# From the tenth pair on, a pair's value products and lane sums issued as one run on TensorE, under a new table of ranks

## The chip, the cores and the metric

One core of one Trainium2 chip runs the whole program. The metric is the device time of one execution in microseconds (us). TensorE (PE) does the matrix products, with a separate weight load (PEld) that overlaps them; VectorE (DVE), ScalarE (ACT) and GpSimd (POOL) do the elementwise work, SyncE (SP) issues every transfer.

## The reference

Four batches of twelve attention heads (448 tokens, 64 columns each) with a soft cap on the scores, then two dense layers with a squared ReLU between them on all 1792 tokens:

```
scores = cap * tanh(scale * q @ k.T / cap)
attn   = exp(scores) / (sum(exp(scores)) + 1e-9)
x      = (attn @ v), heads side by side            # 1792 x 768
h      = x @ w_in                                   # 768 -> 2048
g      = s * relu(h)**2 + b
out    = g @ w_out                                  # 2048 -> 768
```

The weights arrive as float64 and are brought to float32 in the kernel (L655 to L659).

## The kernel before

Heads go in pairs: 4 batches x 6 pairs, 24 in all. A key axis of 448 is cut into three chunks of 128 and a rest of 64; the rests of two neighbouring pairs share a fourth chunk. `scores` (L505) multiplies the keys of one chunk with all queries of both heads of a pair, two matmuls of 64 rows (four for the shared chunk), in f32; ACT takes the tanh out of PSUM (L509) and the exponential in place (L513). Two PSUM buffers (`ps_s`) hold such chunks. `pv` then multiplies the exponentials with the values: for each key chunk four matmuls of 32 columns (L563), and two groups of four that sum the exponentials over the keys with a matrix of ones (L571). One PSUM buffer (`ps_v`) takes these; ACT empties it (L591). Five small transfers, POOL and DVE then turn the sums into a normalised and scaled x, whose largest value is summed over lanes by a small product on PE (L470, once a batch). In the code names below, pair (b, c) is pair c of batch b.

The first dense layer (`m1`, L835 to L837, three f16 products for each f32 one) needs all six pairs of its batch; the second (`m2`, L1086 to L1088) follows. For the last two batches both go by a scheme with fewer products (`m1pair`, `m2pair`, L995). Weight tiles are prepared on the way: `win` does a w_in tile (column sums on PE at L705, a maximum on DVE at L713 to L715, a lane sum at L470, scales at L721 to L726, conversions at L426 to L429, remainders at L446). `wout` does a w_out column tile (maximum at L451, sums on POOL and DVE at L436 and L437, the bias product L778 on PE, a lane sum at L470, scales, a split at L429 and L446 and a transfer away, L819).

The order on every engine is made when the program is built. Each piece of work is entered as an operation with an engine (or several to choose from), a length, a rank, what it reads and what it writes; an entry `at` in the table `CHOICE` gives each unit (a double pair, a weight tile, a column tile of a layer) its rank and step. `emit` then plays the operations through, engine by engine: among the ones at the head of a queue it takes the one that could start first, prefers on PE the kind of the last one (`kind`: 1 and 3 scores, 2 values), and is bounded by `cling`; `bias`, `late` and `lag` are further numbers of that choice. The order that comes out is fixed; at run time each engine works in its own order and waits on semaphores.

An operation of `pv` is one such piece. `parts` says which key chunks go into one: chunks 0 and 1 with the first sums are the first, chunks 2 and 3 with the last sums the second.

## Time and profile before

| | |
|---|---|
| median of 3 runs | 646.98 us (643.51 to 649.58) |
| profiled execution | 644.03 us, span 642.2 us |
| PE busy | 627.1 us, 98% of the span |
| DVE, ACT, POOL busy | 397.6, 326.6, 273.8 us |
| mean granted clock of TensorE | 0.997 |
| moved by DMA | 101.67 MB |

A busy PE in this profile is not PE at its peak: a matmul's record runs on while the next has begun. How fast PE goes is therefore read from starts to starts, as the chain of waits gives them.

### The profile page before, as it was taken

What the parts mean: (1) busy time and instruction counts of PE and PEld (TensorE: products, weight loads), DVE (VectorE), ACT (ScalarE), POOL (GpSimd) and SP (SyncE); (2) the same over time, 40 slices, a digit from 0 to 9 for tenths busy, and PEclk for the clock granted to TensorE, in tenths of its full rate; (3) what the DMA queues carried; (4) which work ended last, traced back from release to release, by engine and by line L of the source; (5) the groups of instructions that cost most, each with busy time, mean ns of one, the idle gap of its engine ahead of it and who ended that gap; (6) DMA issues with size and microseconds to landing.
All of it is one profiled execution on the core that took longest, in us unless ns stands there. A gap on an engine that the chain in (4) does not pass through costs nothing.

```text
span 642.2 us, 11452 instructions
## 1 busy us (share of the span) xinstructions
PE 627.1 (98%) x4404; PEld 331.4 (52%) x4404; DVE 397.6 (62%) x778; ACT 326.6 (51%) x423; POOL 273.8 (43%) x319
## 2 busy tenths in 40 slices
PE   6999999999999999999999999999999999999997
PEld 2333344443334443333544445555558997556997
DVE  5896789997487787787400584745976222666222
ACT  5999987467866547537353561435544001434100
POOL 4553446885566568566343851112834001221000
PEclk9999999999999999989999999999999999999999
DMA  7767355441465674672800216676502875000672
GB/s 289 282 206 216 104 160 157 131 142 47 133 201 153 219 260 122 226 245 83 288 27 1 93 43 234 242 277 212 210 2 68 256 259 168 25 2 3 217 255 72
DMA packets 54775, 101.67 MB, mean 158 GB/s; under 512 B 16193, under 2 KB 34753, under 8 KB 54721
## 3 DMA queue, kind: packets, MB, share of 16 engines
q1 hardware_dynamic: 54720, 100.95, 47.1%
q8 instruction: 34, 0.56, 0.3%
q14 instruction: 21, 0.16, 0.1%
HBM read 82.58 MB, written 18.17 MB: 157 GB/s over the span
## 4 chain that ended last, share of the span: by engine, by line
PE 77%; DVE 8%; DMA 7%; POOL 3%; issue 2%; SPq 1%; ACT 0%; POOLq 0%; ACTq 0%
PE ps_m L995 9%; PE ps_s L505 7%; PE ps_s L995 6%; PE ps_v L563 6%; PE ps_s L836 6%; PE ps_s L837 6%; PE ps_s L835 6%; PE ps_m L1086 5%; PE ps_m L1088 5%; PE ps_m L1087 5%; PE ps_m L835 4%; PE ps_m L837 4%; PE ps_m L836 4%; PE ps_v L571 3%; DMA w<-in_w_in 2%
## 5 line engine op out<-in xcount | busy, mean ns | idle before, releaser
L995 PEld LDWEIGHTS <-w 128*128 128x128 f16 x1008 | 96.6, 98 | 0.7
L509 ACT ACTIVATE bed<-ps_s,arena 128x896 f32<-128x896 f32 x84 | 81.6, 1007 | 16.0 <-PE ps_s L505 14.8
L505 PE MATMUL ps_s<-bed 64*128 64x448 f32 (+1 forms) x384 | 82.7, 590 | 3.3 <-DMA bed<-in_qT 2.6
L513 ACT ACTIVATE bed<-bed,par 128x896 f32<-128x896 f32 x84 | 84.5, 1041 | 0.4
L563 PE MATMUL ps_v<-bed 128*32 128x448 f32 x768 | 82.2, 545 | 0.2 <-ACT pw L591 0.2
L1086 PE MATMUL ps_m<-gt,w 128*128 128x448 f16 x192 | 67.7, 353 | 0.0
L835 PE MATMUL ps_m<-x,w 128*128 128x448 f16 x192 | 67.7, 353 | 0.0
L836 PE MATMUL ps_s<-x,w 128*128 128x448 f16 x192 | 67.7, 352 | 0.0
L1088 PE MATMUL ps_m<-gt,w 128*128 128x448 f16 x192 | 67.7, 352 | 0.0
L837 PE MATMUL ps_m<-x,w 128*128 128x448 f16 x192 | 67.7, 352 | 0.0
L1087 PE MATMUL ps_m<-gt,w 128*128 128x448 f16 x192 | 67.7, 352 | 0.0
L835 PE MATMUL ps_s<-x,w 128*128 128x448 f16 x192 | 67.7, 352 | 0.0
L837 PE MATMUL ps_s<-x,w 128*128 128x448 f16 x192 | 67.7, 352 | 0.0
L836 PE MATMUL ps_m<-x,w 128*128 128x448 f16 x192 | 67.7, 352 | 0.0
L835 PEld LDWEIGHTS <-w 128*128 128x128 f16 x384 | 37.6, 98 | 38.7 <-issue 4.2
L837 PEld LDWEIGHTS <-w 128*128 128x128 f16 x384 | 37.6, 98 | 35.1
L836 PEld LDWEIGHTS <-w 128*128 128x128 f16 x384 | 37.6, 98 | 33.7
L429 POOL TENSOR_SCALAR w<-w 128x512 f32<-128x512 f32 x42 | 35.0, 833 | 40.0 <-DVE w L656 31.9
L930 ACT ACTIVATE pw<-ps_s,arena 128x448 f32<-128x448 f32 x32 | 20.3, 633 | 60.9 <-PE ps_s L837 57.8
L505 PEld LDWEIGHTS ps_s<-bed 64*128 64x128 f32 (+1 forms) x384 | 27.3, 177 | 45.4 <-issue 15.8
L437 POOL TENSOR_TENSOR pw<-pw 128x224 f32<-128x224 f32 x16 | 13.7, 860 | 79.5 <-ACT pw L934 63.1
L563 PEld LDWEIGHTS ps_v<-bed 128*32 128x32 f32 x768 | 20.5, 109 | 52.4 <-issue 38.6
(138 smaller groups left out, 1065.3 us busy)
## 6 DMA issues: line engine op xcount, KB each, us to landing
w<-w SPq DMA_DIRECT2D x48, 512.0 KB, 5.5
w<-in_w_out SPq DMA_DIRECT2D x24, 512.0 KB, 5.5
w<-ws SPq DMA_DIRECT2D x24, 512.0 KB, 4.7
w<-in_w_in SPq DMA_DIRECT2D x18, 512.0 KB, 5.4
bed<-in_v SPq DMA_DIRECT2D x24, 256.0 KB, 3.5
ws<-w SPq DMA_DIRECT2D x12, 512.0 KB, 2.9
bed<-in_kT SPq DMA_DIRECT2D x24, 224.0 KB, 3.8
bed<-in_qT SPq DMA_DIRECT2D x24, 224.0 KB, 3.8
```

What stands on the lines that cost most here:

```text
L429: 0.1 + n * 0.00107, lambda: nc.gpsimd.tensor_scalar(dst(), src(), sc, 1.0, ALU.mult, ALU.mult)
L505: nc.tensor.matmul(P[kp][o, h, 0:S], keys, P[q][rows], start=True, stop=True)
L509: 1.01, rank, lambda: nc.scalar.activation(P[kh], P[kp][:, :, 0:S], AF.Tanh, scale=tsc[:, 0:1]),
L513: 1.04, rank, lambda: nc.scalar.activation(P[kh], P[kh], AF.Exp, scale=par[:, 0:1]), r=["par"], w=[kh],
L563: nc.tensor.matmul(P[kp][o, 0, 0:S], P[kv][:, c, o], prob(c, h), start=(c == 0), stop=(c == NC))
L835: nc.tensor.matmul(ps[:, 0:S], wh, x[:, 0], start=(c == 0), stop=False)
L836: nc.tensor.matmul(ps[:, 0:S], wh, x[:, 1], start=False, stop=False)
L837: nc.tensor.matmul(ps[:, 0:S], wl, x[:, 0], start=False, stop=(c == NP - 1))
L995: nc.tensor.matmul(at(), w(g, zw), b(g, zb), start=g == 0 and x == 0, stop=g == n - 1 and x == 2,)
L1086: nc.tensor.matmul(ps[:, 0:S], wh, ghi[:, f], start=(f == 0), stop=False)
L1087: nc.tensor.matmul(ps[:, 0:S], wh, glo[:, f], start=False, stop=False)
L1088: nc.tensor.matmul(ps[:, 0:S], wl, ghi[:, f], start=False, stop=(f == NF - 1))
```

## The change

From the tenth pair on (`early` is 9; pairs are counted batch by batch), `pv` enters one operation with all four key chunks and both groups of sums instead of two operations. It waits in the planner for the pair's last exponential, and nothing can come between its matmuls. For the first nine pairs the two parts stay. The table of ranks and the numbers `bias`, `late`, `lag` and `cling` are new throughout, so that the order on all engines changes:

```diff
 CHOICE = {
-    'bias': 1.798,
+    'bias': 1.543,
...
-        ('a', 0, 0): (-15.1, 72.6), ('a', 0, 2): (69.2, 7.69), ('a', 0, 4): (78.0, 15.05), ('a', 1, 0): (600.1, 1.25),
+        ('a', 0, 0): (-102.1, 106.63), ('a', 0, 2): (99.7, 0.26), ('a', 0, 4): (189.0, 27.49),
...
-    'late': 0.56,
-    'lag': 0.0,
-    'cling': 21.776,
+    'late': 0.358,
+    'lag': 0.047,
+    'cling': 19.384,
     'parts': ((0, 1), (2, 3)),
+    'early': 9,
...
-        for part in CHOICE["parts"]:
+        for part in CHOICE["parts"] if bb * NP + c2 < CHOICE["early"] else (range(NC + 1),):
             both = part[0] == 0
```

Three places in the order show what it moves. In the rows below a line number of the changed kernel is one higher than that of the same line before (L506 for L505, and so on). The first is PE's queue where the first two pairs of the fourth batch (pairs (3, 0) and (3, 1)) get their values, ahead of the second batch's lane sum (the L470 or L471 row). Before:

```order
L505 MATMUL ps_s<-bed 128x448 x4
L563 MATMUL ps_v<-bed 32x448 x8
L571 MATMUL ps_v<-bed,ones 32x448
L571 MATMUL ps_v<-bed,half 32x448
L571 MATMUL ps_v<-bed,ones 32x448
L571 MATMUL ps_v<-bed,half 32x448
L505 MATMUL ps_s<-bed 128x448 x4
L563 MATMUL ps_v<-bed 32x448 x8
L571 MATMUL ps_v<-bed,ones 32x448 x4
L505 MATMUL ps_s<-bed 128x448 x2
L563 MATMUL ps_v<-bed 32x448 x8
L571 MATMUL ps_v<-bed,ones 32x448
```

and now:

```order
L506 MATMUL ps_s<-bed 128x448 x4
L564 MATMUL ps_v<-bed 32x448 x16
L572 MATMUL ps_v<-bed,ones 32x448 x5
L572 MATMUL ps_v<-bed,half 32x448
L572 MATMUL ps_v<-bed,ones 32x448
L572 MATMUL ps_v<-bed,half 32x448
L506 MATMUL ps_s<-bed 128x448 x8
L564 MATMUL ps_v<-bed 32x448 x16
L572 MATMUL ps_v<-bed,ones 32x448 x5
...
L471 LDWEIGHTS ones_132
L471 MATMUL ps_m<-brief,ones_132 128x1
```

The values of a pair stand in one piece of 16 and 8 matmuls, the scores between two pairs in one of 8 matmuls (four chunks), where halves of values and one or two chunks took turns; in the order before, the lane sum stands four rows and one more chunk behind the last row shown.

The second place is ACT's queue at the same point, where pair (3, 0)'s values are taken out of PSUM (L592; L591 before). Before:

```order
L509 ACTIVATE bed<-ps_s,arena 128x896 x2
L513 ACTIVATE bed<-bed,par 128x896 x2
L591 ACTIVATE pw<-ps_v 128x896
L509 ACTIVATE bed<-ps_s,arena 128x896 x2
L513 ACTIVATE bed<-bed,par 128x896 x2
L509 ACTIVATE bed<-ps_s,arena 128x896
L513 ACTIVATE bed<-bed,par 128x896
L591 ACTIVATE pw<-ps_v 128x896
L509 ACTIVATE bed<-ps_s,arena 128x896
L513 ACTIVATE bed<-bed,par 128x896
```

and now:

```order
L510 ACTIVATE bed<-ps_s,arena 128x896 x2
L514 ACTIVATE bed<-bed,par 128x896 x2
L592 ACTIVATE pw<-ps_v 128x896
L510 ACTIVATE bed<-ps_s,arena 128x896 x2
L514 ACTIVATE bed<-bed,par 128x896 x2
L510 ACTIVATE bed<-ps_s,arena 128x896
L514 ACTIVATE bed<-bed,par 128x896
L510 ACTIVATE bed<-ps_s,arena 128x896
L592 ACTIVATE pw<-ps_v 128x896
```

Between the two emptyings (pairs (3, 0) and (3, 1)) stand the tanh of four chunks now, of three before, and in both orders the first emptying comes ahead of them.

The third place is DVE's queue where a w_in tile's maximum follows the tile before it (the lane sum on PE waits for the CAST to `brief`). Before:

```order
L726 TENSOR_SCALAR arena<-arena 128x1
L659 SCALAR_TENSOR_TENSOR w<-w 128x512
L446 SCALAR_TENSOR_TENSOR w_3_124<-w,arena,w_3_124 128x512 x3
L713 TENSOR_REDUCE arena<-ps_m 128x1
L714 TENSOR_SCALAR arena<-arena 128x1
L715 CAST brief<-arena 128x1
```

and now:

```order
L727 TENSOR_SCALAR arena<-arena 128x1
L428 TENSOR_SCALAR w_3_124<-w,arena 128x512 x2
L447 SCALAR_TENSOR_TENSOR w_3_124<-w,arena,w_3_124 128x512 x3
L714 TENSOR_REDUCE arena<-ps_m 128x1
L715 TENSOR_SCALAR arena<-arena 128x1
L716 CAST brief<-arena 128x1
```

The maximum is that of tile 5 before and of tile 2 now; two conversions of tile 3, which ACT did, stand in DVE's queue ahead of it in the place of a step of another tile.

## Rows read from the trace of the kernel before

**Rows 1.** The page, busy time, share of the span and instructions of each engine

```profile
PE 627.1 (98%) x4404; PEld 331.4 (52%) x4404; DVE 397.6 (62%) x778; ACT 326.6 (51%) x423; POOL 273.8 (43%) x319
```

**Rows 2.** Waits of PE: tile and line, whom for: us, times, longest us

```profile
PE ps_s L505 <- DMA bed<-in_qT: 2.6, 2, 1.9
PE ps_m L778 <- POOL bed L437: 2.5, 1, 2.5
...
PE ps_m L470 <- DVE brief L610: 1.6, 2, 1.4
...
PE ps_m L470 <- DVE brief L715: 0.8, 2, 0.5
```

**Rows 3.** Chain of waits, two stretches: start us, us until the next step

```profile
248.13 1.71 PE ps_s L505 x8
249.84 1.64 PE ps_v L563 x16
...
252.23 1.50 PE ps_v L563 x16
...
281.52 0.29 PE ps_m L1086
281.82 0.19 PE ps_m L1087
```

**Rows 4.** Windows: stretch, length, busy us of PE, PEld, DVE, ACT, POOL, PEclk

```profile
0.00:160.00 160.00, 152.18 (x1123) 59.33 (x1127) 130.55 (x264) 123.62 (x154) 90.65 (x109) 1.00 0.53 174
0.00:300.00 300.00, 288.20 (x2070) 113.04 (x2071) 237.42 (x493) 209.02 (x248) 180.05 (x226) 0.99 0.55 180
```

**Rows 5.** Chain of waits behind 274 us, and the window of 276 to 280

```profile
274.72 3.27 PE ps_s L505 x12
277.99 1.82 PE ps_v L563 x16
...
276.00:280.00 4.00, 4.00 (x28) 1.18 (x28) 3.73 (x9) 2.97 (x4) 3.83 (x7) 0.71 0.38 109
```

**Rows 6.** Timeline: start us, us, instruction [idle before, and for whom]

```profile
105.66 1.00 ACT L509 ACTIVATE bed<-ps_s,arena 128x896 f32<-128x896 f32 x1
106.72 1.02 PE L505 MATMUL ps_s<-bed 64*128 64x448 f32 x4 [0.58 <-ACT bed L509]
...
181.48 0.92 ACT L591 ACTIVATE pw<-ps_v 128x896 f32<-128x896 f32 x1 [0.38 <-PE ps_v L571]
```

**Rows 7.** Timeline of DVE at w_in tiles 3 and 5, and a group by line

```profile
99.49 0.14 DVE L721 COPY arena<-ps_m 128x1 f32<-128x1 f32 x1
...
102.64 0.68 DVE L659 SCALAR_TENSOR_TENSOR w<-w 128x512 int32<-128x512 int32 x1
...
106.68 0.16 DVE L715 CAST brief<-arena 128x1 bf16<-128x1 f32 x1
...
L427 DVE TENSOR_SCALAR w<-w,arena 128x512 f16<-128x512 f32 x7 | 3.2, 491 | 0.0
```

**Rows 8.** Chain of waits, the bias products of w_out from the second on

```profile
199.70 0.31 PE ps_m L778 x2
...
224.13 0.31 PE ps_m L778 x2
...
247.72 0.38 PE ps_m L778 x2
...
274.31 0.38 PE ps_m L778 x2
...
300.54 0.31 PE ps_m L778 x2
```

**Rows 9.** Timeline of the start, SP's queue and PE

```profile
3.54 0.44 SPq L1132 DMA_DIRECT2D par<-in_s  x1
...
4.71 0.65 SPq L481 DMA_DIRECT2D bed<-in_kT  x1
...
12.50 0.97 PE L505 MATMUL ps_s<-bed 64*64 64x448 f32 x4 [1.93 <-DMA bed<-in_qT]
```

58 rows, old and new, of the table CHOICE are left out of this document.

## The prediction

> **What bounds the kernel now.** I read four views. The page's table of engines first: TensorE (PE) is busy for 627.1 of 642.2 us [rows 1], the others for at most 62%. So this kernel ends when PE has worked through its queue, and a change of order can only move what PE loses between matmuls. Second, PE's waits [rows 2]: the longest entry is 2.6 us, and that is the start (L505 for q); four entries make 7.6 us. That seems to leave little. Third, the chain of waits, where each step runs to the start of the next [rows 3]: it shows a loss that "busy" hides. Two score chunks take 1.71 us, and the first half of a value run behind them (L563, two key chunks) takes 1.64; the same half straight behind another half takes 1.50 [rows 3]. So each block of values that follows something else pays 0.14. A value step (one key chunk, four column quarters at once) and a score chunk (two row halves at once) stream the same 448 columns in two passes, so I read half of 1.50, 0.75, for either where nothing changes, and each block of scores pays 1.71 - 1.50 = 0.20. Full-width f16 products run at 0.19 apiece, and the first one behind scores shows 0.29: 0.10 [rows 3]. Fourth, the windows: ScalarE (ACT) is busy 123.6 of the first 160 us, VectorE (DVE) 237.4 of the first 300 [rows 4]. These two set when scores and weights are ready.
>
> **The switches.** No matmul is added or removed: 576 of L563/L571, 192 of L505, 1728 f16 of full width and 1008 of half width stand in both orders. What changes is the number of blocks, counted in PE's order: value blocks 44 to 32, score blocks 51 to 41, blocks of f16 products 17 to 18. At the prices above: 12 x 0.14 = 1.7, plus 10 x 0.20 = 2.0, minus 0.1: **-3.6 us**. The bounds are 0, if what I take for a switch is a wait that comes back elsewhere, and these 3.6.
>
> **Waits that lose their place.** The longest one in mid-run is 2.45 us before the bias product L778 at 274.31, for POOL [rows 2, 8]. Behind it the granted clock is 0.71 in 276 to 280 us, a mean of stretches at 2.4 and 1.2 GHz; two score chunks take 3.27 instead of 1.71 and a first half of values 1.82 instead of 1.64 [rows 3, 5]: 2.45 + 1.56 + 0.18 = 4.2. The lane sums of the batches wait 1.6 (L610, 1.4 of it the second batch's), those of the weight tiles 0.8 (L715) [rows 2], a score chunk 0.58 for its buffer [rows 6]. Sum 4.2 + 1.6 + 0.8 + 0.6 = **-7.2** if all of them go. The second batch's lane sum has a better place now: 54 f16 products (10.3 us), two whole value runs (9.3) and seven score chunks lie between its last pair and it, some 26 us by the prices above, where in the order before they come to 20 us. What may come in the place of the other waits is priced in the next parts; none of it at all would be worth 0, and keeping all of them 7.2.
>
> **Score runs of four.** With the values in one run, four score chunks now stand in a row at four places (three times 8 matmuls of L505 between two value runs, once 2 + 4 + 4 with the shared fourth chunk among them, behind a bias product). Score buffers are two. ACT empties a value buffer in 0.92 and does a tanh in 1.00 [rows 6], and at these places its order has the emptying first. What scores do that must wait for a buffer is in the trace once: a tanh ends at 106.66, the scores start at 106.72 after 0.58 of idling [rows 6]. Worked out from the end of a value run, with ACT 0.2 behind it (an estimate from the 0.38 of idling in that row, which counts from its own last instruction): emptying until 1.1, first tanh until 2.05, second until 3.0. The third chunk, due at 1.7, starts at 2.1; the fourth, due then at 2.85, at 3.05. So 0.6 us a run, four runs: **+2.4**. Bounds: 0 if the emptying is done earlier, 1.05 a run (4.2) if ACT comes half a microsecond later. I take 0.6, as the row of the one such wait gives 0.58. The Trainium skill, page "TensorEngine Tiling", section "PSUM Bottleneck", says that tiling quickens TensorE but not the emptying of PSUM, which may then be the limit. Taken at its word (each of the four chunks at ACT's pace, 0.92 + 4 x 1.00 = 4.9 against 3.2) this would be 1.7 a run and 6.8 in all, so a sum 4.4 us higher; the trace speaks for less, since PE waits for ACT's tanh hardly anywhere.
>
> **Lane sums behind less.** The lane sum of weight tile 2 stands now two score chunks behind its column sums, and DVE reaches its maximum only after finishing tile 3: from the first step of a tile's scales to the end of the next tile's maximum DVE took 99.49 to 106.84 in the trace, 7.35 us, with one step of another tile in it (0.68); in the new order two conversions (0.98) stand there in its place [rows 7]: 7.65 us. PE has 18 products (3.4), the column sums (0.4) and two chunks (1.7) to do: 5.5. That is a wait of 2.1 at most, and none if the scales run quicker than there (they took some 3 of the 7.35); **+1.2**, near the middle, as no row is nearer to one end.
>
> **The weights' pitch.** Each column tile of w_out passes load, DVE, POOL, bias product and a DVE/POOL split before the next one gets its buffers. Bias products follow each other in the trace by 24.4, 23.6, 26.6 and 26.2 us [rows 8]; only the 26.6 ended in a long wait. In the new order PE's own work between the last four is summed by the prices above (48 products 9.2, a value run 4.6, a run of four chunks with its wait 3.8, two chunks 1.7, one 0.95, the bias product and its lane sum 0.3): 3.8 + 9.2 + 4.6 + 3.8 + 0.3 = 21.7, then 25.2, then 22.3. At a pitch of 23.6, the shortest seen, PE waits 1.9 + 0 + 1.3 = **+3.2**. Ends: 0 if the pitch may be shorter than any row shows, and 4.9 + 1.4 + 4.3 = 10.6 at 26.6 throughout. I take 23.6 since no row shows that pitch as a wait, so that the chain can do at least this.
>
> **What else moves.** The rounding of activations goes from DVE to ACT more often (24 tiles instead of 11); that lies behind 300 us, where ACT has 326.6 - 209.0 = 117.6 us of work in 342 [rows 1, 4] and PE waits for none of it: nothing. If that cover were gone, it would be 13 times some 0.6, 7 us. SP's transfers are the same in number and size; what their new places do lies in the pitch above and the start below. The scheduler's own numbers (bias, lag, cling) issue nothing.
>
> **The start.** PE waits 1.93 us for q of the second pair at 12.50; SP began to issue that pair's k at 4.71, behind the small loads of s and b from 3.54 on [rows 9]. These now come after k and q. That is up to 1.17 earlier; the bytes ahead stay the same, so I take **-0.5**, between 0 and -1.2.
>
> **Sum:** -3.6 - 7.2 + 2.4 + 1.2 + 3.2 - 0.5 = -4.5. The profiled execution took 644.03 (span 642.2), 2.95 less than the median of 646.98. So 639.5 against it. The runs shown spread from 643.5 to 649.6, and the profiled one lies at their low end; I add half of the 2.95 for a median: **641 us**.
>
> **Rivals.**
> - Fewer waits than I price: the new order has its slack where the old one waited. Then 644.0 - 3.6 - 7.2 - 0.5 + 1.5 = **634**. For it: PE's waits in mid-run are single places that an order can step round. Against: [rows 6] shows that score buffers do run out. Chance 0.25.
> - DVE keeps the pace. Up to the last bias product at 300.54 DVE is busy 237.4 of 300 us [rows 4, 8], and its work ahead of that product is the same. If its idle stretches (loads, POOL, ACT) stay as long, PE saves its switches only to wait longer, and only the two pairs behind that product gain (2 x 0.34 = 0.7): 644.0 - 0.7 + 1.5 = **645**. This is the case in which the edit does what it says and nothing comes of it. Against: PE waited only once for this chain. Chance 0.17.
> - Slower: the weights' chain at a pitch of 26.6 and PE waiting over 2 us before three bias products, each followed by the lower clock (1.56 + 0.18 = 1.7 as above): 639.5 - 3.2 + 10.6 + 5.1 + 1.5 = **653**. It decides from a pitch of some 25.5 on: 3.8 + 0.3 + 3.2 = 7.3 of waits and one fall of the clock, 9.0 in place of 3.2, bring the time back to 647. For it: 26.6 and 26.2 stand among four pitches. Against: 24.4 and 23.6 do, too. Chance 0.12.
> - My forecast, with a range of its own from 637 to 644: 0.46.
>
> Over 1% faster means below 640.5, about what a measurement of this kernel can tell from no change. A little under half of my own case and the first rival lie there: 0.46. Over 1% slower (653.4) is the upper part of the third rival: 0.05. The rest, 0.49, is within 1%. The range from 632 to 648 leaves out the third rival and a little at the low end.
>
> **What would show it.** A value run should take 4.64 us from its first start to the start behind it (six steps of 0.75 and one switch), where two halves took 2 x 2.39. The four-chunk runs should take 3.8 us; 3.2 says that nothing waits, 4.9 that ACT sets their pace. The bias products should show waits of 1 to 2 us, not 2.45, and PEclk should stay 1.00 through them. The second batch's lane sum should wait for nothing. Wrong would be: DVE idle before the last bias product unchanged at some 63 us, or a PEclk under 0.95 in more than one slice.

## The result, and the profile after

The changed kernel takes 652.67 us (median, 651.64 to 654.16) against 645.99 for the kernel before, measured beside it: a ratio of 1.0111 with a 95% interval of 1.0082 to 1.0140. It is slower by 1.1%, where 641 was forecast. The profiled executions have spans of 651.8 and 642.2 us, so 9.6 more, which is what the traces below have to account for. The mean granted clock fell from 0.997 to 0.987. (One execution scatters: the traced one of chain_first, below, lies 4.7 us over its kernel's median, that of light 3.0.)

The page's table of engines, busy us with the share of the span and the instructions, and its row of the granted clock in 40 slices of 16.3 us:

```profile
PE 631.9 (97%) x4404; PEld 334.6 (51%) x4404; DVE 410.8 (63%) x774; ACT 329.0 (50%) x428; POOL 270.9 (42%) x318
...
PEclk9999799999999997998999999999999999999999
```

Against [rows 1], PE is busy 4.8 us longer with the same matmuls, and three slices are below 9, where a lower clock is granted: around 70, 250 and 305 us. PE's waits in this trace (line waited at, releaser: total, times, longest):

```profile
PE ps_m L779 <- POOL bed L438: 4.5, 2, 4.1
PE ps_m L706 <- POOL bed L696: 2.6, 1, 2.6
...
PE ps_m L779 <- DMA zd<-cmp: 2.1, 1, 2.1
PE ps_m L706 <- DVE bed L695: 1.4, 1, 1.4
PE ps_s L506 <- ACT bed L510: 1.3, 4, 0.4
PE ps_m L471 <- DVE brief L716: 1.0, 2, 0.8
```

Before [rows 2], the longest wait in mid-run was 2.45 us. Now there are three stalls of 2 to 4 us, and they answer to the three slices. PE's instructions at the three places (start, busy time, line, operation, count, in brackets the idle time before it and its releaser):

```profile
65.60 0.20 PE L706 MATMUL ps_m<-ones,bed 128*128 128x1 bf16 x2 [1.38 <-DVE bed L695]
68.45 0.37 PE L706 MATMUL ps_m<-ones,bed 128*128 128x1 bf16 x8 [2.65 <-POOL bed L696]
68.75 3.36 PE L506 MATMUL ps_s<-bed 64*128 64x448 f32 x8
72.04 2.87 PE L564 MATMUL ps_v<-bed 128*32 128x448 f32 x16
...
75.60 0.18 PE L471 MATMUL ps_m<-brief,ones 128*128 128x1 bf16 x1
```

```profile
248.88 0.59 PE L779 MATMUL ps_m<-arena,bed 128*128 128x1 f32 x2 [4.09 <-POOL bed L438]
...
249.43 3.21 PE L564 MATMUL ps_v<-bed 128*32 128x448 f32 x16
```

```profile
301.93 0.38 PE L779 MATMUL ps_m<-arena,bed 128*128 128x1 f32 x2 [2.05 <-DMA zd<-cmp]
...
302.27 2.54 PE L506 MATMUL ps_s<-bed 64*128 64x448 f32 x8
304.74 4.08 PE L564 MATMUL ps_v<-bed 128*32 128x448 f32 x32
...
310.26 0.36 PE L1087 MATMUL ps_m<-gt,w 128*128 128x448 f16 x1
```

A trace counts each f32 matmul twice, so the x8 of scores are two chunks. At the column sums of w_in tile 1, PE waits 4.03 us; two chunks behind it take 3.29 (68.75 to 72.04) instead of 1.71, the half value run 3.56 instead of 2.39 [rows 3]. (The expectations below write 4.4 for this wait; that counts the column sums themselves in.) At the bias product of w_out tile 5 it waits 4.09, and the value run behind takes 7.56 (249.43 to the scores at 256.99) instead of 4.65. At tile 1's it waits 2.05, and two chunks take 2.47 and the value run 5.52 (304.74 to 310.26). So the waits cost 10.2 us and the clock behind them 1.58 + 1.17 + 2.91 + 0.76 + 0.87 = 7.3 more. The windows show the same (stretch, length, busy us of PE, PEld, DVE, ACT, POOL, granted clock, DMA share, GB/s):

```profile
60.00:80.00 20.00, 15.86 (x125) 5.34 (x117) 16.61 (x35) 12.32 (x14) 12.21 (x14) 0.83 0.47 131
240.00:260.00 20.00, 15.55 (x99) 5.07 (x89) 16.92 (x35) 10.22 (x11) 12.47 (x19) 0.83 0.49 155
300.00:320.00 20.00, 18.07 (x111) 7.78 (x112) 11.74 (x26) 8.71 (x9) 9.59 (x14) 0.91 0.78 228
```

0.83 is a mean of stretches at 2.4 and at 1.2 GHz. In the first two windows VectorE is the busiest engine, ahead of PE.

**What held tile 5's bias product.** It sums what GpSimd has added up. GpSimd's queue ahead of it, then VectorE's first step for the tile, then SP's queue ahead of the tile's load:

```profile
235.42 0.87 POOL L430 TENSOR_SCALAR w<-w 128x512 f32<-128x512 f32 x1 [4.19 <-DMA w<-in_w_out]
...
245.11 1.60 POOL L438 TENSOR_TENSOR num<-pw,bed 128x448 f32<-128x448 f32 x1
247.57 1.25 POOL L438 TENSOR_TENSOR bed<-bed 128x256 f32<-128x256 f32 x2 [0.87 <-DVE arena L790]
```

```profile
234.11 0.43 DVE L656 TENSOR_SCALAR w<-w 128x512 int32<-128x512 int32 x1 [2.86 <-DMA w<-in_w_out]
```

```profile
223.65 2.39 SPq L527 DMA_DIRECT2D cmp<-pw  x4
226.14 0.53 SPq L482 DMA_DIRECT2D bed<-in_kT  x1
226.72 0.43 SPq L484 DMA_DIRECT2D bed<-in_qT  x1
227.19 0.90 SPq L648 DMA_DIRECT2D w<-in_w_out  x2
```

The tile's load was issued behind four small transfers and the next pair's k and q, and VectorE had idled 2.86 us, GpSimd 4.19, when it landed. The last adds (247.57) stand behind a head pair's product (245.11, 1.60 us), but that had ended 0.87 us before them: what they waited for last here was VectorE. At tile 1 of w_out the profile names a pair's transfer (`zd`) as the last releaser; the chain of waits behind that runs back to GpSimd's sums for a pair and to the tile's load, issued from 282.70 on. At tile 1 of w_in GpSimd and VectorE convert that tile and two that are wanted later (2 and 3) in turn, and a pair's product stands directly ahead of GpSimd's last square for tile 1 (16.61 of 20 us busy on VectorE).

### The profile page after: what moved, and what is told of

It is laid out like the page before. It is cut to its first block, busy times and chain, and to the rows that moved or that the text cites. A ratio compares the mean times of both kernels' runs of the same rounds, so it can differ in the third digit from the quotient of the medians.

```text
span 651.8 us, 11431 instructions
## 1 busy us (share of the span) xinstructions
PE 631.9 (97%) x4404; PEld 334.6 (51%) x4404; DVE 410.8 (63%) x774; ACT 329.0 (50%) x428; POOL 270.9 (42%) x318
## 4 chain that ended last, share of the span: by engine, by line
PE 64%; DVE 15%; DMA 11%; POOL 3%; issue 3%; ACT 3%; SPq 2%; POOLq 0%
PE ps_m L996 8%; PE ps_s L996 6%; DMA w<-in_w_out 6%; PE ps_s L838 6%; PE ps_s L837 6%; PE ps_s L836 6%; PE ps_v L564 6%; PE ps_s L506 4%; PE ps_m L836 3%; PE ps_m L837 3%; PE ps_m L838 3%; PE ps_m L1087 3%; PE ps_m L1089 3%; PE ps_m L1088 3%; DVE w L447 3%; DVE w L660 3%
## 5 line engine op out<-in xcount | busy, mean ns | idle before, releaser
L564 PE MATMUL ps_v<-bed 128*32 128x448 f32 x768 | 83.9, 572 | 0.9 <-DMA bed<-in_v 0.7
L506 PE MATMUL ps_s<-bed 64*128 64x448 f32 (+1 forms) x384 | 82.8, 593 | 2.0 <-ACT bed L510 1.3
L438 POOL TENSOR_TENSOR pw<-pw 128x224 f32<-128x224 f32 x20 | 19.1, 960 | 103.3 <-ACT pw L935 92.3
L564 PEld LDWEIGHTS ps_v<-bed 128*32 128x32 f32 x768 | 22.6, 114 | 53.9 <-issue 43.7
L506 PEld LDWEIGHTS ps_s<-bed 64*128 64x128 f32 (+1 forms) x384 | 28.0, 179 | 42.2 <-issue 18.0
```

Of the source, the lines that this page charges most:

```text
L506: nc.tensor.matmul(P[kp][o, h, 0:S], keys, P[q][rows], start=True, stop=True)
L564: nc.tensor.matmul(P[kp][o, 0, 0:S], P[kv][:, c, o], prob(c, h), start=(c == 0), stop=(c == NC))
```

## The experiments

My theory: the loss is three waits for prepared weights, each with the lower clock behind it. They come from the new order (the table), and merged runs as such are harmless or a gain. The rival: merging itself costs, since the half value runs had filled PE while scores or weights were late. Apart from these, a question to each wait: is it PE's place that is wrong, the order of a helper's queue, or the amount of work?

### Each half through the planner: merge_only and table_only

merge_only has the old table with merged runs, table_only the new table without:

```diff
 CHOICE = {
+    'early': 9,
...
-        for part in CHOICE["parts"]:
+        for part in CHOICE["parts"] if bb * NP + c2 < CHOICE["early"] else (range(NC + 1),):
```

```diff
-    'early': 9,
+    'early': 24,
```

> The kernel before with the changed line alone: from the tenth pair on a value run is one, and the old table of ranks stays, so that the planner draws the order anew from the old numbers. Theory A (the new order lost the time, at three waits of TensorE: the square sums of w_in tile 1, the bias products of w_out tiles 5 and 1): merging itself pays, 12 value switches of 0.14 and some score switches of 0.20 less, about -3, while the runs over four score chunks cost some 0.8 each; 642 to 646 us, and no wait of over 2 us at a bias product besides those before. Theory B (merging itself: the value run ends later, so the emptying, the pair's transfers and with them the weights' chain are late): a bias product waits over 2 us here too, with a lower clock behind it; 650 us or more.

> The kernel after with every pair's value run cut in two again, the new table of ranks kept. Theory A: the 4.4 us wait at the square sums of w_in tile 1 (before any merged pair) and the low clock behind it stay, about 7 us, the bias products of tiles 5 and 1 wait as in the kernel after, and the switches that merging saved come back, some 3 us; 653 to 658 us. Theory B: the first wait stays, but the bias products of tiles 5 and 1 no longer wait over 2 us, so that of the 12 us lost there most comes back: 642 to 648 us.

Measured: 685.24 (684.72 to 687.56, ratio 1.0629, 1.0607 to 1.0650) and 691.13 (688.23 to 693.09, 1.0723, 1.0701 to 1.0745). One place makes up about half of either loss (the spans are 40.9 and 44.1 us longer). PE's matmuls at the last batch's lane sum in merge_only, 370 to 440 us (count, then busy us and mean ns, then idle time before them, what released the longest, and its us):

```profile
L471 PE MATMUL ps_m<-brief,ones 128*128 128x1 bf16 x2 | 0.3, 165 | 20.4 <-DVE brief L611 20.4
```

Twenty microseconds at the last batch's sum (18.8 in table_only); in merge_only it comes at 411.35, and the last value run starts at 387.71. The planner takes each half as a new problem and comes to an order with a loss that neither kernel has. Nothing follows for either theory: a searched table and the edit that it was searched for can't be told apart in this way. From here on the order that the planner made is kept, and single pieces are moved in it.

### Only the clock: filled

After, with f16 products that nobody reads put where PE would idle: 20 ahead of tile 1's column sums, 18 and 8 ahead of the bias products of tiles 5 and 1:

```diff
+FILL = {"nps": 20, "bps": {5: 18, 1: 8}}
...
+            for _ in range(FILL["bps"].get(d, 0)):
+                nc.tensor.matmul(P[kb][:, 0:S], w1[0][:, 0, 0, 0, 0:128], w1[0][:, 0, 0].rearrange("p a b -> p (a b)")[:, 0:S], start=True, stop=True)
```

> The kernel after with products that nobody reads added on TensorE: 20 of 448 columns in f16 ahead of the square sums of w_in tile 1, 18 ahead of the bias product of w_out tile 5 and 8 ahead of that of tile 1, into the buffer that the real product then overwrites. They take at most the time that TensorE waits there now (20, 18 and 8 times 0.19 us against waits of 4.4, 4.1 and 2.1). If the lower clock behind those waits is the price of the idle time, it stays at full: scores and values behind the first go from 3.29 and 3.56 to 1.70 and 2.39, values behind the second from 7.56 to 4.65, scores and values behind the third from 2.47 and 5.52 to 1.70 and 4.65, -7.3 us in all, 645.4 us, the waits themselves left. If the clock falls there for another reason, or what follows then waits for ScalarE instead: 651 to 654 us.

Measured: 647.38 (645.59 to 649.35), 1.0019 (0.9995 to 1.0042) against before: 5.3 less than after, in spans 8.0 less (643.8). PE at the first place:

```profile
64.49 3.96 PE L706 MATMUL ps_m<-w 128*128 128x448 f16 x20
68.28 0.44 PE L710 MATMUL ps_m<-ones,bed 128*128 128x1 bf16 x12
68.66 1.77 PE L508 MATMUL ps_s<-bed 64*128 64x448 f32 x8
70.36 1.71 PE L566 MATMUL ps_v<-bed 128*32 128x448 f32 x16
```

The column sums come when they came before (68.28), but the scores behind them run at full speed (68.66 to 70.36 is 1.70), and the granted clock is 1.00 at all three places. So the clock behind the waits is shown to cost 5.3 us by the medians, 8.0 by the spans (7.3 were read from the rows), which is most of what the change lost. The waits themselves are still there, as products without use; tile 5's bias product waits 0.79 beside its filler. It isn't a cure, but a measure.

### Moving PE's side alone: moved_three, bias_moved, all_moved

In these, `MOVES` takes single pieces (with what depends on them) past others on one engine's queue: behind the other if they stood ahead of it, else ahead of it. `bps` is a bias product, `ops` its lane sum, `pv` a value run, `m2` a piece of the second layer. bias_moved lets the bias products of tiles 5 and 1 come later; moved_three also brings w_in tile 1's transfers and conversions forward; all_moved is bias_moved with tile 1's column sums later (the lines are from different ones of the three):

```diff
+    ('PE', (('bps', 5), 0), (('pv', 3, 3), 0)),
+    ('PE', (('ops', 5), 0), (('bps', 5), 0)),
+    ('PE', (('m2', 0, 5), 0), (('pv', 2, 2), 0)),
...
+    ('SP', (('wr', 1, 0), 0), ((('cmp', 0, 2), 0, 0), 0)),
...
+    ('PE', (('nps', 1), 0), (('pv', 1, 0), 1)),
```

> The kernel after with its merged runs and its planned order, but for three places. Tile 1 of w_in: its three transfers are issued ahead of the third pair's normalisation transfers, and its conversion on VectorE and GpSimd ahead of that pair's reciprocal. Tile 5 of w_out: bias product and lane sum behind the value run that they stood ahead of, its four output products behind the next value run. Tile 1 of w_out: lane sum behind one score chunk, bias product behind the value run, two f16 blocks ahead of the output products. Theory A: the three waits (4.4, 4.1, 2.1) and the clock behind them (2.8, 2.9, 1.6) go, -12 to -18 us, 635 to 641 us, faster than the kernel before. Theory B: the waits turn up at the next product that needs the same weights, 648 to 653 us.

> The kernel after, in which TensorE does other work that is ready at the two bias products that wait: those of w_out tile 5 behind the value run that followed them, with the four output products behind the next value run, and ScalarE's reading of these behind that run's exponentials; of tile 1 the lane sum behind one score chunk and the bias product behind the value run. If the waits of 4.1 and 2.1 us and the clock behind them (2.9 and 1.6) are the loss of this half: 10 us less by the trace, less what the moved score chunks cost (0.8 to 2), 643 to 646 us. If VectorE's and GpSimd's chain of the weights sets the pace (about 27 us from bias product to bias product), the products only wait elsewhere: 650 us or more.

> As the run with both bias products moved, and the square sums of w_in tile 1 too: on TensorE behind two score chunks and the second value run, their lane sum behind two more score chunks, with VectorE's reading of them put ahead of another tile's conversion, and ScalarE's scaling of that tile behind two exponentials, so that no engine waits in turn for the sums. If the 4.4 us and the clock behind (2.8) are the loss of this half, another 5 to 7 us less: 636 to 640 us, faster than the kernel before. If the pair's normalisation or the weights' chain then stops TensorE at the next product that needs it: as without this move, or slower.

Measured: moved_three 653.18 (651.84 to 654.29, 1.0124, 1.0104 to 1.0144), bias_moved 649.02 (648.73 to 651.54, 1.0076, 1.0042 to 1.0110), all_moved 653.02 (650.91 to 654.49, 1.0110, 1.0074 to 1.0146). In each a wait has gone from where it was and stands elsewhere: in moved_three at a w_in tile's lane sum (5.19), in all_moved at scores (4.58, for ACT) and at a bias product (3.86), in bias_moved at the next w_out tile's bias product:

```profile
273.28 0.59 PE L841 MATMUL ps_m<-arena,bed 128*128 128x1 f32 x2 [4.49 <-DVE bed L499]
```

Asking for the weights later doesn't make them ready sooner; a likely reason, which no run shows by itself, is that the next tile's buffers come free later too. Only bias_moved gains, 3.6 against after by the medians, but its interval and that of after overlap. So a better place on PE alone doesn't remove the waits.

### Merging without the table: joined; the table without merging: split

joined is the kernel before with its order kept; for the twelve pairs that it can be done for, the first half value run is put directly ahead of the second. split is after with its order kept; 13 of its 15 merged runs are cut, the first half two score chunks earlier:

```diff
+                    out[x:y + 1] = [j for j in out[x:y] if j != one and j not in late] + [one, two] + late
...
+    'join': 9,
```

```diff
+            if i in early:
+                self.heads[self.ops[early[i]][3][0]]()
```

> The kernel before with its own planned order, in which on TensorE alone the two value runs of each pair from the tenth on stand together, where the second stood (twelve pairs; with three they did so already); the order of the other engines is that of before, but for one exponential of the last pair. Nothing is planned anew. Theory A (merging pays by itself, the new order lost the time): 8 to 12 value switches of 0.14 and some score switches of 0.20 less, runs of three and four score chunks 0.6 to 0.8 more each where no f16 products stand among them; 643 to 647 us, no new wait of over 2 us at a bias product. Theory B (a later end of the value runs makes the weights' chain late whatever the order): a bias product or a column sum waits 2 us or more with a low clock behind it, 650 us or more.

> The kernel after with its own planned order on all engines, in which TensorE issues the first half of a merged value run (two chunks and their lane sums) two score chunks earlier, at thirteen of the fifteen pairs. Theory A: the waits at the square sums of w_in tile 1 and at the bias products of tiles 5 and 1 stay, since the order of VectorE, GpSimd and the transfers stays; the switches come back, 13 of 0.14 and as many of 0.20 at the most, while four-chunk runs lose their 0.8 each; 651 to 656 us. Theory B: the waits at the bias products of tiles 5 and 1 go or halve, since the score buffers and ScalarE run earlier; 643 to 648 us.

Measured: joined 653.71 (650.53 to 655.40), 1.0126 (1.0088 to 1.0164), so as large a loss as the change's with none of its table. split 649.51 (648.81 to 650.03), 1.0066 (1.0040 to 1.0092): 3.2 less than after, though the two intervals touch. The longest wait of joined (ACT and PE, then the window):

```profile
103.98 1.43 ACT L462 ACTIVATE w<-w,arena 128x512 f16<-128x512 f32 x2 [1.96 <-DVE arena L761]
...
107.98 1.02 PE L541 MATMUL ps_s<-bed 64*128 64x448 f32 x4 [3.18 <-ACT bed L545]
```

```profile
100.00:112.00 12.00, 8.82 (x49) 4.03 (x48) 10.66 (x24) 10.01 (x14) 8.46 (x10) 0.88 0.50 155
```

ACT waits 1.96 for a scale from VectorE, a score buffer stays full, PE waits 3.18, and the clock falls behind that (0.88 in the window). In the kernel before, a half value run of 2.39 us stood there, and the wait was 0.58 [rows 6]. All of joined's score-buffer waits come to 6.3 us in 9 places, before to 0.8 in 2. So a half run saves a switch when merged, but it is also the work that PE has while ACT and VectorE are late. The rival holds for the order of before. In that of after it isn't decided: split gains, but with waits that have moved (tile 5's bias product waits 1.61, tile 1's 4.58), so the gain is no price of merging.

### Less work for VectorE: light and light_split

light is after without two operations in w_in tile 1 and w_out tiles 5 and 1 (those that bring the sign and the lowest bits of a weight into place), in the same order; light_split is light and split together:

```diff
+    'bare': (('wr', 1), ('or', 5), ('or', 1)),
...
+            if bare:
+                nc.vector.tensor_scalar(hi(), hi(), 3, None, ALU.logical_shift_left)
+                return
```

> The kernel after with its order on every engine, in which VectorE does less for three tiles: of w_in tile 1 and of w_out tiles 5 and 1 the two operations that bring the sign and the lowest bits of a weight into place are left out, and the joining one is a plain shift (the weights of these tiles are then wrong in sign and in their last bits). That is 1.1 us and some 0.3 us less on VectorE for each of 11 pieces; every transfer, every buffer and all else stays. If the chain of VectorE and GpSimd is what makes the three products wait: the bias product of w_out tile 5 comes 4 us or more earlier and no longer waits, that of tile 1 neither, the square sums of w_in tile 1 wait 1 to 3 us less, and the clock stays up behind them; 635 to 643 us. If the transfers come too late (issued behind the pairs' normalisation in the same queue): the waits stay within 1 us of 4.4, 4.1 and 2.1; 649 us or more.

> As the run with less of VectorE's work at three tiles (the same operations left out), with the value runs of thirteen merged pairs cut in two again, as in the run named split. There the cut made the kernel after 3 us faster. If that was the weights' chain (the merged run ends later, so that the chain starts later and its bias products wait longer), then with the chain out of the way merged runs pay: this one 1 to 3 us slower than the lighter kernel with merged runs. If it was the score buffers and ScalarE (three and four score chunks in a row), this one is still 1 us or more faster.

Measured: light 647.48 (644.52 to 650.46), 1.0047 (1.0023 to 1.0072); light_split 647.75 (643.68 to 650.66), 1.0043 (1.0011 to 1.0074), not to be told from light. PE in light at the three places:

```profile
65.20 0.35 PE L714 MATMUL ps_m<-ones,bed 128*128 128x1 bf16 x8 [1.39 <-POOL bed L704]
...
245.56 0.42 PE L787 MATMUL ps_m<-arena,bed 128*128 128x1 f32 x2 [4.29 <-POOL bed L439]
...
297.46 0.58 PE L787 MATMUL ps_m<-arena,bed 128*128 128x1 f32 x2 [2.41 <-DVE bed L438]
```

With less to do, w_in tile 1 is waited for 1.39 us instead of 4.03, and the clock stays. The two w_out tiles are waited for as before (4.29 and 2.41), though their conversions are shorter. GpSimd in light ahead of tile 5's bias product:

```profile
243.16 1.13 POOL L439 TENSOR_TENSOR num<-pw,bed 128x448 f32<-128x448 f32 x1 [3.64 <-DMA bed<-zd]
244.24 1.26 POOL L439 TENSOR_TENSOR bed<-bed 128x256 f32<-128x256 f32 x2
```

GpSimd idles 3.64 us for a head pair's transfer (`zd`), with the adds of the weight tile standing behind it in its queue; VectorE's part of that sum had ended at 241.6, so they were ready for some 2.6 us. So the three places point to two causes: at 64 us too much work, at 249 and 302 us the order of queues. Later runs put both to the test.

### Joining where it should fit: join_two

The kernel before, with only pairs (3, 1) and (3, 3) joined and 11 unread products ahead of tile 4's bias product:

```diff
+    'join': ((3, 1), (3, 3)),
+    'fill': {4: 11},
```

> The kernel before with its own order, with two of its pairs merged (the second pair of batch 3 and the fourth, where all the merged runs of the run named joined lost nothing) and 11 products that nobody reads ahead of the one bias product that waits (w_out tile 4, 2.45 us, values 3.27 for 2.39 and scores behind it slow). Filled time at the full clock: -1.7; the two merged pairs: -0.3 for the switches, up to -1.5 if the lane sum's wait of 1.41 beside the first goes with it. 641 to 644 us against 645, ahead of both kernels; if merged runs cost by ScalarE even here: 645 or more.

Measured: 646.65 (644.12 to 649.02), 1.0024 (1.0001 to 1.0046). No gain, even at the two pairs chosen for it.

### The queues of GpSimd and SP: light_num, chain_first, chain_split

light_num is light (its operations left out) with two pieces of GpSimd's moved: a pair's product behind tile 5's last adds, a pair's compact sums behind tile 1's. chain_first leaves nothing out: after with these two moves, with the loads of w_out tiles 5 and 1 ahead of the next pairs' k, q and v, and with tile1_first (below). chain_split is chain_first and split:

```diff
+    ('POOL', (('num', 2, 1), 0), (('cs', 5, 0), 3)),
+    ('POOL', (('cmp', 2, 3), 0), (('cs', 1, 0), 3)),
...
+    ('SP', (('q', 2, 3), 0), (('or', 5, 3), 0)),
+    ('SP', (('k', 2, 3), 0), (('or', 5, 3), 0)),
```

> As the run named light (the same operations of VectorE left out at three tiles), and GpSimd's order changed at two places: the product of the second pair of batch 2 behind the last adds of the column sum of w_out tile 5, and the sums of the fourth pair's compact row behind those of tile 1. In light GpSimd stood 3.6 us at that product for a transfer, with the two adds for the bias product behind it. If that queue is what held the bias product: its wait of 4.29 falls under 0.5, the values behind it take 4.65 and not 7.6, the wait of 2.41 at tile 1 falls under 1; 638 to 642 us. If the transfers of the weights hold it: the wait stays over 3, 646 us or more.

> The kernel after, nothing left out, with the order of the run named tile1_first, GpSimd's two places of the run named light_num, and the loads of w_out tiles 5 and 1 issued ahead of the next pairs' k, q and v and of a store of weights. VectorE was idle for 2.9 us before the first piece of tile 5 had landed, and worked without a gap from there to the sum: with the loads up to 2 us earlier the wait at tile 5 falls from 4.1 to 1 or 2, at tile 1 from 2.05 to under 1, and the clock stays up at one of them at least. 638 to 644 us if the order of the queues is the cause; 649 or more if the transfers' bandwidth is (all of them are still moved).

> As the run named chain_first, with the value runs of the merged pairs cut in two again where that can be (thirteen pairs). In the kernel after the cut alone gave 3 us. If merged runs cost by the score buffers (three and four score chunks in a row): 1 to 3 us faster than chain_first; if only by a late chain: the same or up to 2 us slower.

Measured: light_num 644.74 (642.55 to 647.42), 0.9984 (0.9963 to 1.0006), 2.7 less than light; its tile 5 waits 2.36, between the two answers expected, so GpSimd's queue was a part of it, and tile 1 not at all. chain_first 646.66 (644.72 to 651.32), 1.0023 (1.0001 to 1.0045). SP in it, and PE at tile 5:

```profile
228.78 2.40 SPq L604 DMA_DIRECT2D cmp<-pw  x4
231.28 2.95 SPq L725 DMA_DIRECT2D w<-in_w_out  x4
234.32 0.38 SPq L559 DMA_DIRECT2D bed<-in_kT  x1
```

```profile
250.84 0.38 PE L856 MATMUL ps_m<-arena,bed 128*128 128x1 f32 x2 [0.92 <-POOL bed L515]
```

The weights' load comes ahead of k now, and 4.09 has become 0.92; tile 1 has no wait, though two other w_out tiles have one (2.05 at 192.8, 1.37 at 277.7). The fair comparison is tile1_first (below), which differs by these moves alone: 654.37, with waits of 4.35 and 1.77 at the two tiles. Nothing was left out and no matmul moved, and 7.7 us are gone, so the second cause is shown: the order of the helpers' queues. How much of it was SP's and how much GpSimd's isn't.

chain_split takes 648.98 (646.19 to 650.53; 1.0059, 1.0037 to 1.0082), 2.3 more than chain_first, but the intervals overlap, and its trace has a new wait of 3.09 at tile 1. So cutting the merged runs again gains some 3 us in after, nothing in light, and loses some 2 here, and none of these is well clear of the scatter; only joined's loss is. What merging is worth hangs on the order, and the halves of the change can't be priced apart.

### The stretch at w_in tile 1: tile1_first, both_first, sums_first

Three more orders for 60 to 90 us: tile1_first brings tile 1's later transfers, conversions and squares ahead of those of tiles 2 and 3; both_first does it with fewer pieces ahead of the pairs' own, and has chain_first's other moves; sums_first is both_first with tile 5's scales brought forward too (the lines are from tile1_first, the last from the other two):

```diff
+    ('SP', (('wr', 1, 1), 0), (('z', 0, 2), 0)),
+    ('SP', (('wr', 1, 2), 0), (('z', 0, 2), 0)),
+    ('DVE', ((('wr', 3, 1), 's'), 0), ((('wr', 1, 2), 'f'), 0)),
...
+    ('DVE', (('xm', 0, 4), 0), (('wnm', 1), 1)),
```

> The kernel after, nothing left out, with another order in one place: between the fourth and the sixth pair of batch 0 the two later transfers of w_in tile 1 are issued one pair earlier, and VectorE and GpSimd convert and square its second and third chunk ahead of tiles 2 and 3, whose square sums are wanted 40 us later, and ahead of one pair's reciprocal and product. If the wait at the square sums (1.4 on VectorE, 2.65 on GpSimd) is an order in which other tiles and pairs stand ahead: the wait goes and the clock stays up behind it, 5 to 7 us less than after, 646 to 648 us. If the pairs' normalisation held back stops the value runs in turn (three buffers for emptied runs): 650 us or more, with waits of value runs between 55 and 80 us.

> The kernel after, nothing left out, with the orders of chain_first for w_out tiles 5 and 1 and a better one for w_in tile 1. In tile1_first and chain_first its square sums no longer waited, but a value run did (1.4 to 2.0 us, for a product of GpSimd that frees the emptied run's buffer) and then the lane sum (3.5 us, for VectorE's reading of the square sums, which still stood behind another tile's conversion). Here that product stands where it stood in the kernel after, ahead of the third chunk's conversion, and VectorE reads the sums, and takes the root behind them, ahead of the conversions of tiles 2 and 3. If the queues' order is the cause of all three waits: both go, with the low clock behind them, 5 to 8 us less than chain_first, 638 to 642 us, faster than the kernel before. If the work of VectorE and GpSimd is too much for this stretch in any order, a wait of 3 us or more turns up by 90 us: 646 us or more.

> The kernel after, nothing left out, with the orders of both_first and, between the square sums of w_in tile 1 and the lane sum of batch 0, VectorE's reading of tile 5's square sums and both tiles' roots ahead of the conversions of tile 3, and the last pair's reciprocal ahead of the roots. In both_first the square sums of tile 1 and their lane sum no longer waited; the next lane sum (tile 5) did, 5.4 us, with values at 4.64 for 2.39 behind it, since VectorE read that tile's square sums behind the conversions of tile 3. If the order of the queues is all: that goes too and no wait over 2 us is left before 100 us; 640 to 643 us, faster than the kernel before. If the amount of work is: 3 us or more are waited at the lane sum of tile 5 or at that of batch 0; 646 us or more.

Measured: tile1_first 654.37 (653.89 to 655.42; 1.0143, 1.0114 to 1.0171), both_first 647.90 (646.59 to 650.74; 1.0051, 1.0028 to 1.0074), sums_first 652.38 (649.49 to 653.65; 1.0092, 1.0058 to 1.0126). The column sums wait 0.38 at most; in their place a lane sum does, in tile1_first tile 1's (3.48, behind a value run's 1.36), in both_first tile 5's, in sums_first the first batch's:

```profile
80.50 0.16 PE L554 MATMUL ps_m<-brief,ones 128*128 128x1 bf16 x1 [5.38 <-DVE brief L799]
```

```profile
88.96 0.16 PE L559 MATMUL ps_m<-brief,ones 128*128 128x1 bf16 x1 [4.48 <-DVE brief L699]
```

The first batch's lane sum came at 78.5 us before, with w_in tiles 2, 0 and 1 ahead of it. The new table puts 4, 0, 1 and 5 ahead of it, and it comes at 87.8. Before, then after:

```profile
78.47 0.16 PE L470 MATMUL ps_m<-brief,ones 128*128 128x1 bf16 x1 [0.17 <-DVE brief L610]
```

```profile
87.82 0.18 PE L471 MATMUL ps_m<-brief,ones 128*128 128x1 bf16 x1
```

In the other orders of this stretch it comes between 88.1 and 90.6, in light at 83.8. That speaks for one more tile's work of VectorE and GpSimd, not for its order. It was never moved out of the stretch whole, so this isn't settled.

### What was understood, together: chain_filled

After with GpSimd's moves and the loads first, and, since order didn't help at tile 1, its old order with 20 unread products:

```diff
+    ('POOL', (('num', 2, 1), 0), (('cs', 5, 0), 3)),
...
+    ('SP', (('k', 2, 3), 0), (('or', 5, 3), 0)),
...
+    'fill': {1: 20},
```

> The kernel after with the order that helped (the loads of w_out tiles 5 and 1 ahead of the next pairs' k, q, v and a store of weights; on GpSimd a pair's product and another pair's compact sums behind the column sums of these tiles), w_in tile 1 left in the order of the kernel after, and its wait of 4.4 us filled with 20 products that nobody reads, so that the clock stays up behind it. In chain_first the bias product of tile 5 waited 0.9 and that of tile 1 not at all, with the full clock behind both: against after that is 3.2 + 2.9 and 2.0 + 1.6 less, with 1.4 more at tile 2; the clock behind the square sums is 2.8. By these rows some 11 us less than after, 641 to 644 us, at or a little under the kernel before. If the order of the queues at the w_out tiles gave nothing by itself, as filled: 647.

Measured: 644.32 (642.39 to 645.91), 0.9975 (0.9955 to 0.9996): a quarter of a percent under before, 1.3% under after, at a clock of 1.00. Tile 5's bias product waits 0.87 in it, tile 1's not at all, and it is 3.1 us faster than filled, so the queues' order is worth something beyond the clock. This is the fastest version that leaves nothing out, and the gain over before is at the edge of what can be measured.

## Why the prediction was wrong

Point by point, against its own sum of -4.5:

- **Switches, -3.6.** The price was right: a value run takes 4.65 us (277.75 to 282.40 in the rows below), forecast 4.64. The sum was not measured by itself: no run shows that merging gains clear of the scatter, and joined, 9.6 us slower than the kernel before beside it, shows what it can take. The half runs had a second use, as work for PE while ACT and VectorE are late, which the sum priced at nothing.
- **Score runs of four, +2.4.** Right in kind, a quarter too small. The waits are 0.35, with ACT's tanh as the releaser, and three of the runs take 3.98, some 4.05 and 3.98, where 3.8 was forecast and 3.2 would be free of waits. The reading that the prediction tried of the Trainium skill (page "TensorEngine Tiling", section "PSUM Bottleneck"), each chunk at ACT's pace and so 4.9 a run, isn't borne out.

```profile
273.44 1.77 PE L506 MATMUL ps_s<-bed 64*128 64x448 f32 x8
275.57 1.92 PE L506 MATMUL ps_s<-bed 64*128 64x448 f32 x8 [0.35 <-ACT bed L510]
277.42 0.38 PE L779 MATMUL ps_m<-arena,bed 128*128 128x1 f32 x2
...
277.75 3.21 PE L564 MATMUL ps_v<-bed 128*32 128x448 f32 x32
...
282.40 0.98 PE L506 MATMUL ps_s<-bed 64*64 64x448 f32 x8
```

- **Lane sums.** Tile 2's +1.2 did not come. Two other tiles' lane sums wait 1.0 together. The second batch's waits for nothing, as forecast.
- **Start, -0.5.** The first values start at 12.53, before at 13.40: -0.9.
- **Waits that lose their place, -7.2.** The old ones went, as said. (The four entries that the prediction adds up from [rows 2] make 7.5, not 7.6.) This is the first step that failed: it listed the waits that go and, for those that come, looked at score buffers, lane sums and bias products alone. The column sums of w_in tiles, with 1.24 of waiting before, are not among its rows and were put at no change; they became 4.03 with 2.75 of clock, 5.5 more. The row of before:

```profile
67.05 0.35 PE L705 MATMUL ps_m<-ones,bed 128*128 128x1 bf16 x8 [1.24 <-POOL bed L695]
```

  The table's four tiles ahead of the first batch's lane sum, instead of three, stood in the new order to be read.
- **The weights' pitch, +3.2 at 23.6.** The second, and the larger. Bias products followed each other by 27.1, 33.3, 26.4, 28.5 and 24.5 us, none by 23.6 [rows 8 for before]. PE's own work between the last four was right: the gaps less their waits and the clock are 22.3, 25.6 and 22.5, where 21.7, 25.2 and 22.3 were forecast. What failed is when the weights are ready. A pitch read from the old order was taken for a property of the chain, but it is set by the queues that the chain passes through, and the change reorders those; in chain_first the first and the last of these three gaps are 23.2 and 22.4. And the two long waits, 4.09 and 2.05, brought 2.9 and 1.6 of lower clock: 11.1 with 0.4 of a short wait, so 7.9 more. The fall of the clock had been priced (1.74 behind 2.45) as a saving only, and in the third rival; the forecast's own waits were left free of it.

-4.5 + 5.5 + 7.9 = 8.9, and the small misses together (0.8 + 1.0 - 1.2 - 0.4) are 0.2: 9.1, where the spans differ by 9.6. Part of that closeness is luck, since the switches stand in it unmeasured.

Nearest was the third rival, 653 with a chance of 0.12: waits of over 2 us for weights, each followed by the lower clock. It had them at three bias products; they were at two, and one at a w_in tile. The rival in which VectorE keeps the pace was half right: in the stretch at 60 to 90 us it seems to (light). Of the signs named beforehand, PEclk fell below 9 tenths in three slices, one of the two that were to say "wrong". The other was VectorE's idling ahead of the last bias product, some 63 us before. It is 54.7 now, as the window until there shows (columns as in the windows above), against [rows 4]; so VectorE did not idle as long as before, but it was busy longer, in as many instructions.

```profile
0.00:302.00 302.00, 285.45 (x2016) 113.80 (x2016) 247.35 (x493) 201.77 (x239) 173.30 (x221) 0.98 0.54 177
```

Still open: whether w_in tile 1's stretch has too much work or only no good order among those tried, and what merging is worth in an order made for it throughout.

## What to carry to other kernels

When an order changes, list the waits that may come as carefully as those that go, and price each with the time at the lower clock behind it, which was here 70% of the waits' own. For each chain that the critical engine waits for, read what stands ahead of its pieces in the in-order queues of the helpers (a transfer queue, GpSimd): two moved pieces and a few loads issued sooner took a wait of over 4 us to 0.9. A short run between others may be the filler that hides another engine's lateness; ask what covers that before merging it.

## What the runs showed of the hardware

- The clock's price: behind idle times of TensorE of 2.05, 4.03 and 4.09 us the same work took 1.6, 2.8 and 2.9 us longer, the granted clock a mean between 2.4 and 1.2 GHz. Behind 0.9, 1.4 and 1.6 us of idling in other runs, value runs took 4.65 as ever, but so did the one behind 2.36 us in light_num (245.15 to 249.80, granted clock 1.00 from 244 to 250), while 2.05 us brought the lower clock in after: the length of one idle stretch doesn't decide it by itself.
- Products that nobody reads, in the place of the idling, kept 2.4 GHz and gave back 5.3 us of the median (8.0 of the span).
- Two operations less for each piece of three weight tiles (light) made the kernel some 5 us faster, though VectorE is busy for 63% of the span: its share of the whole run said nothing of the 20 us in which it was the busiest engine.
